# The sum of all branches in two column groups of 224 instead of four of 112, in a single-core decode kernel

## The chip, the cores and the metric

The kernel runs on one core of a Trainium2 chip. The metric is the time on the device in microseconds (us), from runs without a profile; the profile's own span is a little shorter. Before the change the median of three runs is 189.18 us (189.01 to 189.19), and the profiled execution has a span of 187.2 us.

## What is computed

One decode step: two batch rows of width 448 go through a layer normalization without weights, and then through two branches in parallel, whose results are added to the input.

```
xn  = layernorm(x)                              # x: (2, 1, 448) bf16
q   = xn @ wq                                   # 16 query heads of 256
k,v = last 4096 positions of the caches         # 8 kv heads of 256, each for 2 query heads
A   = softmax(q k^T / 16) v  @ wo               # (2, 1, 4096) @ (4096, 448)
h   = xn @ w1 + b1                              # 448 -> 1792
B   = (h * tanh(softplus(h))) @ w2              # 1792 -> 448
out = x + A + B                                 # (2, 1, 448) bf16
```

Nearly all bytes are those of the two caches: 2 batches x 8 heads x 4096 positions x 256 values in bf16 for each of k and v.

## The kernel before

**Staging.** The kernel walks over four units `u`, each of two kv heads in both batches (J = 4 streams). Per unit, two loads of 4096 KB bring k and two bring v; one of 896 KB brings the rows of `wo` that belong to the unit's heads. All big loads are issued from one queue (SyncE) in the order in which the program writes them, into a ring of three buffers. `wq`, `w1` and `w2` go through the same ring. The order of all engines is written out by hand (lines 568 to 614), with no planner.

For a unit, VectorE transposes k in 32x32 blocks (`turns`, line 269), TensorE forms the scores (line 356), ScalarE takes their exponentials (line 364), VectorE transposes them into `p` (line 367), and TensorE sums p times v (line 402). The result is gathered from its column groups (line 420), scaled by the softmax's denominator (line 447), and spread by products with a 0/1 matrix into the layout `ox` (lines 461 and 473), with which eight matmuls on `wo` add the unit's share of A to the output.

**Where the output is summed.** For units 0 to 2 these eight matmuls (`mix_early`, line 482) add into `early`, a PSUM tile of 2 x 448 that also begins with x (line 229). For the last unit everything goes into a second PSUM tile, `acc`:

- `carry` (lines 234 to 245) copies `early` to SBUF on ScalarE and brings it into `acc` with a 2x2 identity in fp32. It stands ahead of the last unit's `values`.
- `mix` (called at line 612, through `add_rows`) adds the last unit's eight rows of `wo`.
- `dense_out` adds the fourteen rows of `w2` (a "row" is here one product of a 128x2 stationary operand with 448 columns). `w2` arrives in four parts of 7, 4, 2 and 1 rows; the last three are the very last loads of the kernel.

**Column groups.** `acc` is 128 partitions x 112 columns. Row sums of two batches need only two partitions; the 448 columns are cut into G = 4 pieces of DG = 112, and piece g lies at partitions 32g and 32g+1. [...]`add_rows` (lines 247 to 256) makes four matmuls of a row, each with the same two stationary columns and another quarter of `rows`, into another column group (trace line 249).

**The end.** Four copies bring `acc` together in `res` (2 x 448, bf16): pieces 0 and 2 by VectorE (line 621), 1 and 3 by ScalarE (line 623). One transfer (line 624) writes `res` to the output, after which the program's closing synchronization runs.

Of the kernel before, what the change touches and what calls it, by code (L numbers as in the profile page):

```python
# [12 lines left out]
FP32 = mybir.dt.float32  # L13
# [4 lines left out]
def kernel(  # L18
# [14 lines left out]
    P = 128  # L33
    G = 4
# [4 lines left out]
    Bsz, Sq, D = A_x.shape  # L39
    _, Hkv, Sk, Dh = A_k_cache.shape  # L40
    HqDh = A_wq.shape[1]
    Hq = HqDh // Dh
    rep = Hq // Hkv
# [16 lines left out]
    NCH = HW // P  # L60
    F2 = F // 2
    NI = F2 // P
    DG = D // G
    assert Sq == 1 and Bsz == 2 and rep == 2 and Dh == 256 and G * DG == D and Hq == 16
    assert W == 4096 and D == 448 and F == 1792
    scale = float(Dh) ** -0.5

# [14 lines left out]
    ps_a = ctx.enter_context(tc.tile_pool(name="ps_a", bufs=1, space=PSUM))  # L82
# [146 lines left out]
    nc.tensor.matmul(  # L229
        early[:], lhsT=ident[0:Bsz, 0:Bsz], rhs=x_bf[:], start=True, stop=False  # L230
    )
    acc = ps_a.tile([P, DG], FP32)

    def carry():
        e_sb = small.tile([P, 2 * Dh], FP32, tag="vs", name="e_sb", bufs=1)[0:Bsz, 0:D]
        nc.scalar.copy(out=e_sb, in_=early[:])
        for g in range(G):
            nc.tensor.matmul(
                acc[32 * g : 32 * g + Bsz, :],
                lhsT=id2[:],  # L240
                rhs=e_sb[:, g * DG : (g + 1) * DG],
                start=True,
                stop=False,
                skip_group_check=True,
            )

    def add_rows(lhsT, rows, stop=False):
        for g in range(G):
            nc.tensor.matmul(  # L249
                acc[32 * g : 32 * g + Bsz, :],  # L250
                lhsT=lhsT,
                rhs=rows[:, g * DG : (g + 1) * DG],
                start=False,
                stop=stop,
                skip_group_check=True,
            )
# [233 lines left out]
    def mix(u):  # L490
        ox = state.pop(("ox", u))
        w = wo_t.pop(u)[:].rearrange("p k h (c d) -> p (k h c) d", c=2)
        for i in range(8):
            add_rows(ox[:, i, :], w[:, i, :])
# [65 lines left out]
    def dense_out(part):  # L560
        k, lo, hi = w2_parts[part]
        for i in range(lo, hi):
            at = k * KH + i * D
            add_rows(
                act_bf[:, i, k, :], state["w2"][:, at : at + D], stop=(k == 1 and i == NI - 1)
            )
# [34 lines left out]
    for part in range(len(w2_parts)):  # L601
        load_w2(part)
    carry()
    values(u, 0)
    values(u, 1, 40)
# [8 lines left out]
        dense_out(part)  # L614

    res = consts.tile([Bsz, D], BF16)
    for g in range(G):
        dst = res[:, g * DG : (g + 1) * DG]
        src = acc[32 * g : 32 * g + Bsz, :]
        if g % 2 == 0:  # L620
            nc.vector.tensor_copy(out=dst, in_=src)
        else:
            nc.scalar.copy(out=dst, in_=src)
# [31 lines left out]
```

The softmax here doesn't subtract the row's maximum and nothing guards it: scores larger than these inputs give would overflow.

## Time and profile before

| what | before |
|---|---|
| time, median of 3 | 189.18 us |
| profile span | 187.2 us |
| mean granted TensorE clock | 0.717 |
| bytes read from HBM | 77.67 MB, 415 GB/s over the span |
| busy: TensorE matmul, VectorE, ScalarE | 78.2, 92.7, 12.6 us |
| matmuls into `acc` in the tail | 88, from 182.01 us on |
| one of these, from start to end | 298 ns (median) |
| copy of 2x112, VectorE and ScalarE | 266 and 244 ns (mean) |
| issue of the output transfer | 185.20 us |

How to read it: busy time of an engine is the union of its instructions' times, and matmuls overlap, so the duration of one (298 ns) says little of how often one can start. The chain of waits is the profile's way back from the last instruction to what released each step. "Granted clock" is the share of TensorE's full clock that it was given; it changes in steps over the run. Stretches of time are counted in us from the start of the span.

### The profile page before, as it was taken

To read this page: it belongs to the slowest core of one execution; us is meant where nothing else is said; L and a number is where in the kernel's file an instruction comes from. 1 tells how busy PE (TensorE), PEld (TensorE's weight loads), DVE (VectorE), ACT (ScalarE), POOL (GpSimd) and SP (SyncE) were. 2 spreads that over 40 slices of the span, in tenths; PEclk is the share of its full clock that TensorE was granted. 3 is DMA by queue.
4 is the path that set the end of the run, shared out by engine and by line. 5 is a ranking of instruction groups with operands and counts; after the bars stand their busy time and mean duration, and the time that the engine had idled before them with its cause. 6 is when DMAs were issued, how large, how long until landed. Compare 5 with 4: busy or idle time off the path is not lost.

```text
span 187.2 us, 1951 instructions
## 1 busy us (share of the span) xinstructions
PE 78.2 (42%) x852; PEld 35.3 (19%) x852; DVE 92.7 (50%) x94; ACT 12.6 (7%) x27; POOL 4.9 (3%) x16
## 2 busy tenths in 40 slices
PE   0453014793219200882049002870067004855684
PEld 0211001551003000440012001420022002422283
DVE  6604397984792098038930395048920593040021
ACT  3003000101000100110000100110001000120101
POOL 8100000000000000000000000000000000000000
PEclk9999999958555855698556755897557555996555
DMA  6999999999999999999999999999999999999991
GB/s 218 420 476 441 427 434 387 454 438 448 441 427 420 403 443 404 464 434 448 441 420 424 413 441 417 451 431 448 434 434 420 413 441 427 441 413 416 417 407 42
DMA packets 4195, 77.78 MB, mean 416 GB/s; under 512 B 470, under 2 KB 732, under 8 KB 1628
## 3 DMA queue, kind: packets, MB, share of 16 engines
q1 hardware_dynamic: 4184, 77.67, 97.0%
q8 instruction: 6, 0.10, 0.2%
q14 instruction: 1, 0.01, 0.0%
q10 hardware_dynamic: 4, 0.00, 0.0%
HBM read 77.67 MB, written 0.00 MB: 415 GB/s over the span
## 4 chain that ended last, share of the span: by engine, by line
DMA 62%; PE 17%; DVE 15%; issue 3%; ACT 1%; SPq 0%; DVEq 0%
DMA v<-in_A_v_cache_dram 30%; DMA k<-in_A_k_cache_dram 15%; DVE kt L269 12%; DMA w<-in_B_w_dram 11%; DMA wq<-in_A_wq_dram 6%; PE pv L402 5%; PE sc L356 3%; PE h_ps L519 2%; PE o L420 1%; DVE p L367 1%; PE acc L249 1%; PE dn L380 1%; PE q_ps L291 1%; PE o L435 1%; DVE rec L388 1%
## 5 line engine op out<-in xcount | busy, mean ns | idle before, releaser
L269 DVE STREAM_TRANSPOSE kt<-k 128x4096 f32<-128x4096 f32 x16 | 70.1, 4420 | 33.9 <-DMA k<-in_A_k_cache_dram 33.9
L402 PE MATMUL pv<-v,p 128*32 128x512 bf16 x244 | 25.5, 590 | 72.3 <-DMA v<-in_A_v_cache_dram 72.3
L356 PE MATMUL sc<-kt,qd 128*32 128x512 bf16 x256 | 20.8, 463 | 13.3 <-DVE kt L269 13.3
L402 PEld LDWEIGHTS <-p 128*32 128x32 bf16 x244 | 9.2, 133 | 86.7 <-issue 63.4
L356 PEld LDWEIGHTS <-qd 128*32 128x32 bf16 x256 | 7.4, 109 | 25.5 <-issue 20.5
L364 ACT ACTIVATE ex<-sc 128x512 bf16<-128x512 f32 x8 | 4.8, 597 | 89.6 <-PE sc L356 89.6
L447 DVE TENSOR_TENSOR oT<-o,rec 128x16 bf16<-128x16 f32 x4 | 0.7, 174 | 20.4 <-PE o L420 18.1
L367 DVE STREAM_TRANSPOSE p<-ex 128x512 bf16<-128x512 bf16 x8 | 5.2, 690 | 10.6 <-ACT ex L364 10.6
L388 DVE TENSOR_REDUCE rec<-dn 128x8 f32<-128x512 f32 x4 | 2.8, 692 | 13.5 <-PE dn L380 13.5
L414 ACT COPY vs<-pv 128x512 f32<-128x512 f32 x4 | 2.3, 585 | 56.5 <-PE pv L402 56.5
L420 PE MATMUL o<-sel,vs 128*128 128x8 f32 x32 | 5.2, 289 | 2.1 <-ACT vs L414 2.1
L482 PE MATMUL early<-wo,ox 128*2 128x448 bf16 x24 | 5.0, 352 | 1.9 <-ACT ox L473 1.9
L420 PEld LDWEIGHTS o<-sel,vs 128*128 128x128 f32 x32 | 4.8, 228 | 4.6 <-ACT vs L414 4.6
L380 PE MATMUL dn<-p,ones 128*128 128x512 bf16 x8 | 3.2, 491 | 3.8 <-DVE p L338 3.8
L291 PE MATMUL q_ps<-wq,xs 128*32 128x512 bf16 x28 | 3.8, 623 | 2.3 <-DMA wq<-in_A_wq_dram 1.9
L519 PE MATMUL h_ps<-xs,w 128*128 128x4 bf16 x49 | 3.7, 196 | 1.3 <-DMA w<-in_B_w_dram 1.3
L345 PE MATMUL sc<-mneg,ident 128*128 128x512 bf16 x8 | 4.1, 516 | 0.0
L308 DVE COPY qT<-qt_ps 128x16 bf16<-128x16 bf16 x4 | 0.4, 165 | 7.1 <-PE qt_ps L303 7.1
L212 PE MATMUL xr_ps<-ident,xrows 2*128 2x2 bf16 x7 | 1.0, 181 | 6.7 <-DVE xrows L211 6.7
L519 PEld LDWEIGHTS <-w 128*128 128x128 bf16 x49 | 3.2, 150 | 1.5 <-DMA w<-in_B_w_dram 1.4
L482 PEld LDWEIGHTS <-ox 128*2 128x2 bf16 x24 | 1.8, 83 | 4.1 <-ACT ox L473 2.2
L212 PEld LDWEIGHTS <-xrows 2*128 2x128 bf16 x7 | 0.7, 99 | 6.9 <-DVE xrows L211 6.7
(68 smaller groups left out, 44.9 us busy)
## 6 DMA issues: line engine op xcount, KB each, us to landing
k<-in_A_k_cache_dram SPq DMA_DIRECT2D x8, 4096.0 KB, 27.9
v<-in_A_v_cache_dram SPq DMA_DIRECT2D x7, 4096.0 KB, 21.3
wq<-in_A_wq_dram SPq DMA_DIRECT2D x2, 1792.0 KB, 9.2
wo<-in_A_wo_dram SPq DMA_DIRECT2D x4, 896.0 KB, 18.9
v<-in_A_v_cache_dram SPq DMA_DIRECT2D x1, 2560.0 KB
w<-in_B_w_dram SPq DMA_DIRECT2D x1, 1568.0 KB, 21.2
v<-in_A_v_cache_dram SPq DMA_DIRECT2D x1, 1024.0 KB, 22.0
w<-in_B_w_dram SPq DMA_DIRECT2D x1, 784.0 KB, 22.2
```

What stands on the lines that cost most here:

```text
L269: nc.vector.transpose(out=kt[i][:, :, r, :, :], in_=t[:, r * KE : (r + 1) * KE].bitcast(FP32).rearrange("p (a c j) -> p a c j", c=P // (R ...
L291: nc.tensor.matmul(q_ps[32 * u : 32 * (u + 1), :], lhsT=xs[:, s, :], rhs=wq_t[s][:, u * 512 : (u + 1) * 512], start=(s == 0), stop=(s == N ...
L345: nc.tensor.matmul(sc[:].rearrange("p t c m -> p (t c m)"), lhsT=ident[:], rhs=mneg[:].rearrange("p a j -> p (a j)"), start=True, stop=Fal ...
L356: nc.tensor.matmul(sc[32 * w : 32 * (w + 1)].rearrange("p t c m -> p t (c m)"), lhsT=qd[:, u, 2 * n + e, :, :].rearrange("p g q -> p (g q) ...
L364: nc.scalar.activation(out=ex[:, :, :, i, :], in_=sc[:], func=ACT.Exp, scale=scale)
L367: nc.vector.transpose(out=p_all[:, :, h * TH : (h + 1) * TH, :].rearrange("p g t q -> p t g q"), in_=ex[:, h * TH : (h + 1) * TH].rearrang ...
L380: nc.tensor.matmul(dn[:].rearrange("p a q -> p (a q)"), lhsT=ones[:], rhs=p_run[:, i].rearrange("p t q -> p (t q)"), start=(i == 0), stop= ...
L388: nc.vector.tensor_reduce(out=rec[:], in_=dn[:].rearrange("p a q -> p q a"), axis=AXIS.X, op=ALU.add)
L402: nc.tensor.matmul(pv[32 * w : 32 * (w + 1), :, :].rearrange("p x d -> p (x d)"), lhsT=p_run[:, g, 4 * a : 4 * a + 4, :].rearrange("p t q ...
L420: nc.tensor.matmul(po[:, c, :], lhsT=sb[:, x, c::2], rhs=sel[:, x, :], start=(x == 0 and c == 0), stop=(last and x == 1), skip_group_check ...
L482: nc.tensor.matmul(early[:], lhsT=ox[:, i, :], rhs=w[:, i, :], start=False, stop=(u == U - 2 and i == 7),)
L519: nc.tensor.matmul(h_ps[:, i, :, :].rearrange("p k b -> p (k b)"), lhsT=w1_v[:, s, i, :], rhs=xs[:, s, 0 : 2 * Bsz], start=False, stop=(s ...
```

## The change

`acc` becomes 128 x 224: the 448 columns are cut into SG = 2 pieces of SD = 224, at partitions 0 and 32. `carry` and `add_rows` make two matmuls of twice the width where they made four, and two copies of 224 columns, one on VectorE and one on ScalarE, replace the four of 112. It is meant to shorten the end: fewer instructions on TensorE, and one copy on each engine instead of two in a row. What is computed, and the order in which rows are added, stay the same.

```diff
+    SG, SD = 2, D // 2
-    acc = ps_a.tile([P, DG], FP32)
+    acc = ps_a.tile([P, SD], FP32)
 
     def carry():
         e_sb = small.tile([P, 2 * Dh], FP32, tag="vs", name="e_sb", bufs=1)[0:Bsz, 0:D]
         nc.scalar.copy(out=e_sb, in_=early[:])
-        for g in range(G):
+        for g in range(SG):
             nc.tensor.matmul(
                 acc[32 * g : 32 * g + Bsz, :],
                 lhsT=id2[:],
-                rhs=e_sb[:, g * DG : (g + 1) * DG],
+                rhs=e_sb[:, g * SD : (g + 1) * SD],
...
     def add_rows(lhsT, rows, stop=False):
-        for g in range(G):
+        for g in range(SG):
             nc.tensor.matmul(
                 acc[32 * g : 32 * g + Bsz, :],
                 lhsT=lhsT,
-                rhs=rows[:, g * DG : (g + 1) * DG],
+                rhs=rows[:, g * SD : (g + 1) * SD],
...
     res = consts.tile([Bsz, D], BF16)
-    for g in range(G):
-        dst = res[:, g * DG : (g + 1) * DG]
+    for g in range(SG):
+        dst = res[:, g * SD : (g + 1) * SD]
         src = acc[32 * g : 32 * g + Bsz, :]
```

More of the change, by code (lines that the diff above doesn't have):

```diff
@@ L62 @@
     NI = F2 // P
-    DG = D // G
-    assert Sq == 1 and Bsz == 2 and rep == 2 and Dh == 256 and G * DG == D and Hq == 16
+    assert Sq == 1 and Bsz == 2 and rep == 2 and Dh == 256 and Hq == 16
     assert W == 4096 and D == 448 and F == 1792
```

## The prediction

> **What bounds the kernel now.** I read the page first, then the chain of waits, then the tail in order of time, then busy time by stretches.
>
> ```profile
> PE 78.2 (42%) x852; PEld 35.3 (19%) x852; DVE 92.7 (50%) x94; ACT 12.6 (7%) x27; POOL 4.9 (3%) x16
> ...
> PEclk9999999958555855698556755897557555996555
> DMA  6999999999999999999999999999999999999991
> ...
> HBM read 77.67 MB, written 0.00 MB: 415 GB/s over the span
> ```
>
> The DMA row is at 9 in every slice but the first and the last: until about 182 us the kernel is bound by its reads, and no work of TensorE, VectorE or ScalarE matters unless it delays a read. The change touches almost only what comes after, so the question is what the last 5 us are made of. The last three digits of PEclk are 5: in the tail the matmuls have half the clock, which I take as 1.2 GHz (why, below).
>
> The chain of waits, its last pieces in order of time (start, length, what):
>
> ```profile
> 181.69 0.19 DVE ox L473
> 181.88 0.14 issue
> 182.01 1.98 PE acc L249 x76
> 183.99 0.02 issue
> 184.01 0.57 PE acc L249 x12
> 184.58 0.25 DVE res L621
> 184.83 0.30 DVEq L650
> ```
>
> The matmuls into `acc` are the chain: 88 of them from 182.01 to 184.55, then the copies to `res`. The last piece, named by a drain, covers each engine's second copy, as the timeline shows:
>
> ```profile
> 182.01 0.92 PE L249 MATMUL acc<-wo,ox 128*2 128x112 bf16 x32 [0.36 <-DVE ox L473]
> ...
> 182.71 1.83 PE L249 MATMUL acc<-w,act_bf 128*2 128x112 bf16 x56
> ...
> 184.57 0.56 DVE L621 CAST res<-acc 2x112 bf16<-2x112 f32 x2 [2.71 <-PE acc L249]
> 184.61 0.51 ACT L623 CAST res<-acc 2x112 bf16<-2x112 f32 x2 [2.76 <-PE acc L249]
> 185.20 0.28 SPq L624 DMA_DIRECT2D out_dram<-res  x1
> ```
>
> The 32 matmuls on `wo` (8 rows of four) start in the 0.70 us from 182.01 to 182.71. Instruction by instruction, the four of a row start within 10 ns of one another and each next row 93.4 ns later (182.152, .245, .338, .432 ...). 112 columns at 1.2 GHz are 93.3 ns. So the four column groups stream at the same time, and a row of 448 columns costs the time of 112.
>
> Is the tail held by TensorE or by the last pieces of `w2`? The stretches of this line tell (length, PE busy and count, PEld busy and count, clock, DMA share, GB/s):
>
> ```profile
> 182.71:182.99 0.28, 0.28 (x24) 0.28 (x16) 0.50 0.42 160
> 182.99:183.27 0.28, 0.28 (x24) 0.28 (x16) 0.50 0.42 154
> 183.27:183.55 0.28, 0.28 (x24) 0.23 (x16) 0.50 0.32 118
> 183.55:183.83 0.28, 0.28 (x20) 0.26 (x10) 0.50 0.25 86
> 183.83:184.11 0.28, 0.26 (x16) 0.10 (x8) 0.50 0.04 13
> 184.11:184.39 0.28, 0.28 (x12) 0.16 (x5) 0.50 0.00 0
> ```
>
> Both. Up to 183.3 the rows come as fast as TensorE streams them. Then the count falls from 24 to 12 while the DMA runs out: the three small parts of `w2` land at 183.41, 183.97 and 184.24 (their semaphores), and the rows that use them start at 183.45, 184.01 and 184.28, some 40 ns after. Streamed without a wait, the 22nd row would end at 182.263 + 21 x 0.0934 = 184.22; it ends at 184.54. So 0.32 us of the tail is waiting for data, and that is all the slack that slower matmuls can use.
>
> **What the Trainium skill says.** All four places are in "TensorE: Matmul & The Clock Gate". "Back-to-back issue gap" gives columns/1.2 ns at the half clock, columns/2.4 plus 2.5 ns at the full one. The trace agrees at both ends: 93.4 ns for 112 columns here, and in the third early product at line 482, at a granted clock of 1.00, 189 ns from start to start for 448 columns in one group (448/2.4 + 2.5 = 189.2). Part 3, "The mechanism", says that products in different column tiles run at once; the four starts within 10 ns agree. Part 1, "Wait — 56ns, not 53.3ns?", puts a floor of about 25 ns from start to start under small matmuls; here starts lie 2 to 7 ns apart within a row and 23.3 ns on average, so the trace contradicts that floor for matmuls in different column groups. Part 1, "What's actually happening", says the clock is released after about 3.4 us of busy array. Of this trace: TensorE is busy almost without a gap from 174.6 to 184.6, and the clock stays at 0.50.
>
> **The change part by part.**
>
> Fewer, wider matmuls. A row becomes 2 matmuls of 224 columns in 2 groups: 44 instead of 88 in the tail, in the same 22 rows. The columns of a group double: 224/1.2 = 186.7 ns a row instead of 93.4, if the two groups stream together. No row of before has two groups, but its neighbours bound it: 448 columns in four groups cost 112 columns' time, in one group 448 columns' time. If nothing of the two overlapped, a row would cost 373 ns; if the issue of instructions were what counts, 2 x 23.3 = 47 ns. I take 187, since both neighbours follow columns per group over clock to 1%.
>
> The tail, then: `ox` is ready as before, first row at 182.01. Its 252 ns become 252 + 93 = 345, so it ends at 182.357; the 22nd ends 21 x 0.1867 = 3.92 us later, at 186.28. Where are the waits for `w2`? The part of 4 rows is wanted at row 16, at 182.01 + 15 x 0.187 = 184.81 (landed 183.41); that of 2 rows at 185.56 (183.97); the last at 185.93 (184.24). All are there, so the 0.32 us of waiting goes. From 184.54 to 186.28: **+1.74 us**, which is 22 x 0.0934 = 2.05 of extra streaming less 0.32 of slack. All on the path: nothing but these matmuls leads to the copies.
>
> Half the weight loads (44 fewer of 80 to 128 ns): they already lie beside the matmuls, since rows keep to 93.4 ns. Nothing.
>
> The copies. Each engine does one of 2x224 in place of two of 2x112. VectorE took 266 ns for 112 and, at line 324, 420 ns for 256 elements a partition from PSUM in fp32: 1.07 ns an element, so 266 + 112 x 1.07 = 386 ns. ScalarE took 244 for 112 and 521 for 448 (line 236): 0.82 an element, 336 ns. Before, the second copies end at 185.135 and 185.119, 0.563 and 0.513 after the first ones start. After, the later is VectorE, 0.386. Saved: 0.563 - 0.386 = **0.18 us**, on the path, since the output waits for both. Bounds: 0.10, if the wider copy also pays something for its width, to 0.25.
>
> `carry` (line 238): 4 fp32 products in two passes each become 2 of twice the width. It takes 0.37 us at 167.21 now; streamed in half as many groups it takes perhaps 0.2 us more. The pieces of `values` behind it on TensorE wait for `v` for 4.6 us in two waits, the longer 3.48, which leaves 1.1 for the one after `carry`. Hidden.
>
> The size of `acc` in PSUM (896 bytes a partition) is nothing in time; the output transfer is the same.
>
> Sum: +1.74 - 0.18 = +1.56 us. 189.18 + 1.56 = **190.7 us**, 0.8% slower.
>
> **The rivals.**
>
> 1. *The rows stay hidden, and the kernel is faster.* If issuing instructions sets the pace, or the landing of `w2`, the end stays at the last landing plus one row, 184.24 + 0.3, and only the copies count: 189.0. For it: the last three pieces of the tail do wait for a landing, and the starts average 23 ns. Against: the slack is 0.32 us, while doubling the stream asks 2.05; and the 93.4 ns between rows is the streaming time to the nanosecond, with gaps of 2 ns inside a row.
>
> 2. *The clock rises in the longer tail.* 4.3 us without a gap might bring it to 1.00. The clock changes in steps of 3.41 us; the next steps would fall at 183.54 and 186.95. If it rose at 183.54, the 2.74 us left would halve: 189.18 + 1.56 - 1.37 = 189.4. Against: in the 3.4 us ahead of that step the array is filled with columns far less than at 94.8 to 98.2 us, where 20 matmuls of 512 columns in four groups did not raise it; with two groups in use it is filled less still than before.
>
> 3. *Two groups don't overlap as four do*, in whole: 22 x 0.373 = 8.2 us for the rows, so 186.28 + 4.1, and 194.8 us. Against: nothing in either neighbour hints at it.
>
> **How the numbers follow.** Forecast 0.88, rival 1 0.05, rival 2 0.05, rival 3 0.02. In the forecast the spread is that of the copies (0.15 in all), some 0.1 for the fill of the first row, and 0.2 for medians of runs (the three of before lie within 0.18): 190.35 to 191.1. This leaves out the rivals, 0.12, and some 0.05 of the forecast, so it holds about 0.83. Slower by over 0.2% means over 189.56: 0.88 + 0.02 + part of rival 2 = 0.92. Within: 0.03, the rest of rival 2. Faster: 0.05, rival 1.
>
> **What would show it.** Right: 44 matmuls into `acc` in the tail, rows 187 ns apart, at a clock of 0.50 with two starts close together; no wait for `w2` between them; their end near 186.3; one copy of about 386 ns on VectorE and 336 on ScalarE. Rows 93 ns apart would refute the sum, and point to the clock or to a pace of issue; rows 373 ns apart to rival 3. A clock of 1.00 in the last two slices of the page is rival 2. The prediction fails too if the reads before 182 us take another time, which nothing in the change should cause.

## The result, and the profile after

The changed kernel takes 190.73 us (median of 6 runs, 190.08 to 191.04) against 189.12 us before (6 runs): a ratio of 1.0082, 95% interval 1.0066 to 1.0098. It is slower by 1.6 us; forecast were 190.7 us. Medians here and below are of all runs of a kernel, while ratios leave out the executions more than 1.5% above its fastest, of which only the runs with added products have any.

The page's rows for the clock and the transfers, of the changed kernel:

```profile
PEclk9999999958555855798556655896558555998555
DMA  6999999999999999999999999999999999999980
```

The clock is again at 5 in the last three slices. The DMA row now ends with an 8 and a 0: the stretch after the last read, 2.9 us before, has become nearly as long as a slice of the page (4.5 of 4.7 us).

Its tail in order of time (start, length, engine, line, operation):

```profile
182.31 1.66 PE L249 MATMUL acc<-wo,ox 128*2 128x224 bf16 x16 [0.36 <-DVE ox L473]
...
183.76 2.82 PE L249 MATMUL acc<-w,act_bf 128*2 128x224 bf16 x28
186.61 0.38 DVE L621 CAST res<-acc 2x224 bf16<-2x224 f32 x1 [4.45 <-PE acc L249]
186.65 0.34 ACT L623 CAST res<-acc 2x224 bf16<-2x224 f32 x1 [4.50 <-PE acc L249]
187.06 0.28 SPq L624 DMA_DIRECT2D out_dram<-res  x1
```

Half as many matmuls take longer: 44 from 182.312 to 186.581, 4.27 us, where 88 took 2.53. Instruction by instruction the two of a row start 2 ns apart, and rows follow every 186.7 ns (182.639, .826, 183.012, .199 ...). Nothing waits for `w2` any more. By stretches (length, PE busy and count, PEld busy and count, clock, DMA share, GB/s):

```profile
182.99:183.27 0.28, 0.28 (x8) 0.20 (x4) 0.50 0.58 221
184.11:184.39 0.28, 0.28 (x8) 0.20 (x4) 0.50 0.08 26
185.51:185.79 0.28, 0.28 (x6) 0.19 (x4) 0.50 0.00 0
```

Before, the count fell where the DMA ran out. Here the rows keep their 186.7 ns with DMA at 221 GB/s and at 0 (a count of 8 or 6 is where the stretch cuts the rows): TensorE alone sets the pace.

The two profiled spans differ by 1.86 us (187.17 and 189.03), and the time of the output's issue by as much (185.198 and 187.057). It divides almost without a rest: the first row starts 0.30 later (182.011 and 182.312), because the reads of this execution landed later (the last part of `w2` at 184.239 and 184.559); the rows take 4.269 - 2.532 = 1.74 more; from the first copy's start to the issue it is 0.443 instead of 0.626, 0.18 less. The 0.30 belongs to the execution and not to the change: in a later profile of the same changed kernel (below) the first row started at 181.975.

### The profile page after: what moved, and what is told of

Read it like the earlier page. It is cut to its first block, busy times and chain, and to the rows that moved or that the text cites. A ratio compares the mean times of both kernels' runs of the same rounds, so it can differ in the third digit from the quotient of the medians.

```text
span 189.0 us, 1853 instructions
## 1 busy us (share of the span) xinstructions
PE 80.2 (42%) x804; PEld 36.0 (19%) x804; DVE 93.0 (49%) x93; ACT 12.4 (7%) x26; POOL 4.7 (2%) x16
## 4 chain that ended last, share of the span: by engine, by line
DMA 64%; DVE 15%; PE 14%; issue 3%; SPq 1%; ACT 1%
DMA v<-in_A_v_cache_dram 32%; DMA k<-in_A_k_cache_dram 15%; DVE kt L269 12%; DMA w<-in_B_w_dram 11%; DMA wq<-in_A_wq_dram 6%; PE pv L402 4%; PE sc L356 3%; PE acc L249 2%; PE h_ps L519 2%; DVE p L367 1%; PE q_ps L291 1%; DVE rec L388 1%; PE dn L380 1%; ACT ex L364 1%; SPq L105 1%
## 5 line engine op out<-in xcount | busy, mean ns | idle before, releaser
L356 PE MATMUL sc<-kt,qd 128*32 128x512 bf16 x256 | 21.4, 471 | 13.3 <-DVE kt L269 13.3
L249 PE MATMUL acc<-w,act_bf 128*2 128x224 bf16 x28 | 2.8, 392 | 0.0
```

The source lines that it names most:

```text
L249: nc.tensor.matmul(acc[32 * g : 32 * g + Bsz, :], lhsT=lhsT, rhs=rows[:, g * SD : (g + 1) * SD], start=False, stop=stop, skip_group_check= ...
L356: nc.tensor.matmul(sc[32 * w : 32 * (w + 1)].rearrange("p t c m -> p t (c m)"), lhsT=qd[:, u, 2 * n + e, :, :].rearrange("p g q -> p (g q) ...
```

## The experiments

The theory: the rows of the tail cost *columns per group / granted clock*, and the clock is at half there. A column group is here the place, at partitions 32g, to which one matmul of a row writes; 112 columns in 93.4 ns are 1.2 columns a ns at a granted clock of 0.50, so 2.4 at 1.00. Rivals: a price per matmul or per group whatever the clock; the landing of `w2` as the true end; the copies as the larger part.

**One group of 448.**

```diff
-    SG, SD = 2, D // 2
+    SG, SD = 1, D
```

> The change carried one step further: one group of 448 columns, 22 matmuls, one copy of 448 on VectorE. My theory is time by columns per group over clock: 373 ns a row at half clock, 22 x 0.187 = 4.1 us more than two groups, and a copy of 266 + 336 x 1.07 = 0.63 us in place of 0.39: 190.73 + 4.1 + 0.24 = 195.1 us if the clock stays at 0.50 throughout. The tail is then 8 us long, and if so long a stream brings the clock up after some 5 us, it is 193 to 194. A theory of a fixed price per matmul gives less than two groups: under 190 us.

193.38 us; ratio 1.0221 (1.0207 to 1.0235). The stretches of the tail, columns as above:

```profile
184.00:187.00 3.00, 3.00 (x9) 1.01 (x8) 0.50 0.00 0
187.78:189.12 1.34, 1.34 (x7) 0.42 (x5) 1.00 0.00 0
```

At 0.50 the rows start 373 ns apart, twice the 186.7 of two groups, with half the matmuls again. At 187.78, after 5.9 us of this stream, the clock went to 1.00 and the last rows follow every 189 ns. So the time is below the 195.1 of a constant clock, within the 193 to 194 that were given for a rise. A price per matmul is refuted: 88, 44 and 22 matmuls for the same rows take 2.5, 4.3 and 7.2 us. The one copy of 448 took 614 ns (0.63 expected).

**Three rows less, with two groups and with four.** Both leave out 3 of the 8 rows of the last unit's product with `wo`; that part of the sum is not computed.

```diff
     def mix(u):
...
-        for i in range(8):
+        for i in range(5):
```

> Two column groups as in the changed kernel, but the last unit's product with wo leaves out 3 of its 8 rows (that part of the sum is not computed). My theory: the tail is a stream of 22 rows at 187 ns with no wait, so 3 rows less take 0.56 us off: 190.73 - 0.56 = 190.2 us, and all 19 rows still follow at 187 ns. If the landing of w2 held the end, nothing would be gained: 190.7 us.

> The kernel before with the same 3 rows of wo left out. My theory: in this kernel the 0.32 us of waiting for the last parts of w2 take up what 3 rows less (0.28 us) would give, since the end is the last landing and one row: 189.1 us, no change, the waits in front of the small parts growing instead. If streaming alone set the end, it would be 189.12 - 0.28 = 188.85 us.

Two groups: 190.04 us, ratio to the kernel before 1.0039 (1.0027 to 1.0051), so 0.7 us under the full change, where 0.56 was expected. Its profile has 19 rows in 3.710 us against 22 in 4.269, 0.559 less, which is 3 x 186.7 ns; its tail started late (183.13) with late reads, and this execution was the slowest of the 22 (191.08 us), so only the length is compared. The clock's row of its page shows one thing more, in its last digit:

```profile
PEclk9999999958555965555857955579559855589657
```

The 7 is a clock that rose to 1.00 at 187.12, 0.28 us after the last row had ended.

Four groups: 189.07 us, 0.9993 (0.9983 to 1.0002), no change that can be told. What the rows gave went into a longer wait, now visible in the order of time:

```profile
182.55 0.87 PE L249 MATMUL acc<-w,act_bf 128*2 128x112 bf16 x28
183.59 1.10 PE L249 MATMUL acc<-w,act_bf 128*2 128x112 bf16 x28 [0.17 <-DMA w<-in_B_w_dram]
```

The second part of `w2` landed at 183.545, and its first row began at 183.588. The same three rows are free in the kernel before and cost their full streaming time after: the tail has gone from waiting for data to being TensorE's.

**The clock raised, first try.** Products that nobody reads, in a PSUM tile that is free by then, while TensorE waits for `v`; added to the change and to the kernel before. `warm(n)` makes n of them, each 128x128 by 512 columns; its definition is left out here.

```diff
     carry()
+    warm(4)
     values(u, 0)
+    warm(14)
     values(u, 1, 40)
```

> Two column groups, with 4 products of 128x128 by 512 columns that nobody reads ahead of the last unit's first values and 14 ahead of its second ones, where TensorE waits for v (1.1 and 3.5 us). They are to keep the granted clock up into the tail. My theory: the loss is streaming at half clock, 224 columns a group; at a clock of 1.00 a row takes 93 ns, the stream falls under the landing of w2, and only the shorter copy is left: 189.12 - 0.18, about 188.9 us. If the loss is per matmul or per column group whatever the clock, it stays near 190.7 us. If the added products run at half clock they end late and delay the tail by up to 3 us; the profile would show it.

> The kernel before with the same 18 added products. My theory: the tail ends with the landing of the last part of w2 plus one row, so a higher clock brings at most the shorter last row, 0.05 us: 189.1 us. A theory in which the clock sets the end of this kernel too has 22 rows at 47 ns, and 1.0 us less for them: 188.1 us.

Two groups: 190.55 us, ratio 1.0062 (1.0048 to 1.0076), not the 188.9 expected. The profile tells why: the clock stayed up until 181.32, fell ahead of the tail, and came back at 184.73, in the midst of it:

```profile
182.00:184.70 2.70, 2.66 (x30) 1.88 (x32) 0.50 0.37 135
184.77:185.60 0.83, 0.83 (x18) 0.51 (x12) 1.00 0.00 0
```

Up to 184.7 the rows are 187 ns apart, after it 96: both values of the theory in one tail (224/1.2 and some 2.5 ns more than 224/2.4). So the price is not one per group whatever the clock. The run failed as a remedy.

Four groups: 189.91 us, 1.0044 (1.0028 to 1.006), where 189.1 was expected. Rows of 48 to 49 ns are there while the clock is up (it fell at 182.90), and they wait for `w2`. But inside the 20th row TensorE stops, waiting for no semaphore:

```profile
184.87 0.44 PE L249 MATMUL acc<-w,act_bf 128*2 128x112 bf16 x9 [0.43 <-issue]
```

From start to start the gap is 0.68 us. What it is stayed open. The DMA records show no fetch of instructions within it; the last large one ended at 183.61.

**The clock raised up to the tail.** The same, with more products where TensorE waits for the last pieces of `v`.

```diff
     gather(u, last=False)
+    warm(6)
     values_fixed(u, 1, 40, 56)
+    warm(1)
     values_fixed(u, 1, 56, TV)
```

> Two column groups and the 18 added products ahead of the values, with 6 more behind the gather and 1 between the last two pieces of values, where TensorE waits for v, so that no 3.4 us ahead of the tail are idle. Theory: at a clock of 1.00 through the tail a row takes 96 ns (as the last rows did in the run with 18 products after its clock rose), the rows meet the landing of w2 again, and the tail from its first row to the end of the last takes 2.5 to 2.6 us in place of 4.27: 189.0 us. If the clock does not hold, each row at half clock adds 0.09 us.

> The kernel before with the same 25 added products. Theory: rows of 48 ns, but the end is the landing of the last part of w2 plus a row, so 189.1 us if nothing else happens. In the run with 18 products there was a gap of 0.68 us inside a row with no semaphore waited for, which made it slower than before (189.9 us): if that gap belongs to the added instructions, it returns here, and the time is 189.8 us again.

Two groups: 189.12 us, ratio 0.9992 (0.9976 to 1.0008). With the clock up, as in the profile of one of the nine faster runs (188.79 to 189.78), the whole loss is gone. The clock's row of the page, and the tail by stretches:

```profile
PEclk9999999957555855699555755798557655899999
```

```profile
182.90:183.18 0.28, 0.28 (x12) 0.25 (x8) 1.00 0.42 160
183.18:183.46 0.28, 0.28 (x12) 0.26 (x8) 1.00 0.37 141
183.46:183.74 0.28, 0.28 (x10) 0.20 (x6) 1.00 0.40 144
183.74:184.02 0.28, 0.28 (x10) 0.25 (x8) 1.00 0.17 58
184.02:184.30 0.28, 0.26 (x8) 0.09 (x4) 1.00 0.05 16
184.30:184.58 0.28, 0.28 (x6) 0.18 (x5) 1.00 0.00 0
```

Rows are 96 ns apart, and the falling count of the kernel before is back: parts of `w2` land at 183.651, 184.214 and 184.485, and their rows start 41 or 42 ns after each. The tail lasts 2.593 us. It is no remedy to keep: in four of the 13 executions, with a lower mean clock (0.733 to 0.750 against 0.763 to 0.781), the time was over 193 us. No trace of those was taken; the expectation of the first try named the likely way, products at half clock that end late.

Four groups: 189.42 us, 1.0019 (1.0002 to 1.0036), the fastest 188.92. In its profile the clock fell at 183.14, after four rows 48 ns apart; the rest are 93.4 apart, and the first row had started only at 182.98, since the added products ended late. The gap of the first try isn't there. So this run doesn't show what four groups do with the clock up throughout.

**The changed kernel again.**

> The changed kernel itself, beside the three others on the same chip: 190.7 us, rows 187 ns apart wherever the granted clock is 0.50. In an execution where the clock rises before the tail has ended, the rows after that take 96 ns and the time is shorter by 0.09 us for each of them; such executions would be the fastest of its runs.

190.49 us (6 runs, 189.77 to 191.29), ratio 1.0073 (1.0054 to 1.0092). Its profile has rows of 186.7 ns at 0.50 throughout, and a tail of 4.268 us. All 12 runs of the changed kernel by their mean granted clock:

```
0.721  191.29                      0.738  190.50 190.56 190.64
0.725  190.49 190.53 190.82 190.82 0.746  190.08 190.08
0.729  191.04                      0.764  189.77
```

On the whole the time falls as the clock rises. In 73 runs of the kernel before, from 0.694 to 0.812, it doesn't: 188.92 at the lowest clock, 189.18 to 190.28 at the highest. The 22 runs of two groups with three rows less divide too: the five at 0.764 and above took 189.43 to 189.58 us, the others 189.82 to 191.08. That fits a tail that has come to depend on the clock. Whether the clock rose within the tail of the fast ones is not seen, as their traces weren't kept.

**Two groups, four copies.** Each engine copies its group in two halves of 112.

```diff
-        dst = res[:, g * SD : (g + 1) * SD]
-        src = acc[32 * g : 32 * g + Bsz, :]
+        for h in range(0, SD, SD // 2):
+            dst = res[:, g * SD + h : g * SD + h + SD // 2]
+            src = acc[32 * g : 32 * g + Bsz, h : h + SD // 2]
```

> Two column groups, but four copies of 112 columns, two on each engine, as before the change. My theory: the copies' part of the change is 0.18 us of gain, so undoing it gives 190.73 + 0.18 = 190.9 us, with the output transfer issued some 0.63 us after the first copy starts instead of 0.44. A rival in which the second copy is hidden gives 190.7 us.

190.69 us (4 runs, 190.41 to 190.81); 1.0081 (1.0067 to 1.0095). Too coarse for 0.2 us, but the profile has the intervals: from the first copy's start to the issue 0.507 us, where one copy each takes 0.443 and the kernel before 0.626. So undoing the copies loses 0.064 of the 0.183, and 0.12 comes from something else than their number.

```profile
186.38 0.44 DVE L622 CAST res<-acc 2x112 bf16<-2x112 f32 x2 [4.45 <-PE acc L249]
186.41 0.39 ACT L624 CAST res<-acc 2x112 bf16<-2x112 f32 x2 [4.50 <-PE acc L249]
```

Two copies of 263 and 252 ns lie in 0.44 us: the second starts 191 ns after the first, before the first has ended.

**Four groups, the last copied first.** In the kernel before each second copy waits for TensorE's semaphore once more, in the run above not. Here the order lets the wait go.

```diff
-    for g in range(G):
+    for g in reversed(range(G)):
         dst = res[:, g * DG : (g + 1) * DG]
```

> The kernel before with the four copies in the other order: groups 3 and 2 first, then 1 and 0. TensorE ends the groups in the order 0 to 3, so the second copy of each engine needs no wait of its own any more. In the run with two groups and four copies such second copies started 0.15 to 0.19 us after the first; in the kernel before, with a wait each, 0.29 and 0.27. Theory: the copies take 0.51 us from the first start to the issue of the output in place of 0.63, but start up to 0.07 us later, as group 2 and 3 are signalled 34 and 68 ns after group 0: 0.05 us less, 189.05 us. If instead the number of copies was the price, nothing changes: 189.1 us.

189.07 us; 0.9998 (0.999 to 1.0006), and 0.608 us from the first copy to the issue.

```profile
184.63 0.54 DVE L621 CAST res<-acc 2x112 bf16<-2x112 f32 x2 [2.71 <-PE acc L249]
184.67 0.50 ACT L623 CAST res<-acc 2x112 bf16<-2x112 f32 x2 [2.75 <-PE acc L249]
```

My explanation falls: without the wait the second copy still starts 282 ns after the first (294 with it), so the wait is worth some 0.02 us. What is left as the difference is the place: these two copies read different partitions, while those that overlap read the same ones, at columns that adjoin. That the partitions are what counts was not tried alone.

**Four groups, one copy an engine.** The four copies and the one transfer make room for the lines below; the lines that go are left out.

```diff
+    nc.vector.memset(acc[:], 0.0)
...
+    res = consts.tile([P, DG], BF16)
+    nc.vector.tensor_copy(out=res[0:64, :], in_=acc[0:64, :])
+    nc.scalar.copy(out=res[64:P, :], in_=acc[64:P, :])
+    flat = out.flatten_outer_dims().rearrange("b (g c) -> b g c", g=G)
+    for b, engine in enumerate((nc.sync, nc.scalar)):
+        engine.dma_start(out=flat[b], in_=res[b : b + 97 : 32, :])
```

> Four column groups of 112 as before, but one copy on each engine: VectorE takes partitions 0 to 63 (two groups) in one copy of 64x112, ScalarE partitions 64 to 127, after a memset of the PSUM tile at the start; the output goes out in two transfers, one a batch row, from two queues. My theory: streaming stays at 93 ns a row, and the copies lose the second of each pair, 0.563 - 0.266 = 0.30 us: 188.8 us. If the two transfers cost more than one, up to 0.3 us comes back: 189.1 us.

190.1 us; 1.005 (1.0036 to 1.0064): slower than before, not faster.

```profile
185.24 0.27 DVE L618 CAST res<-acc 64x112 bf16<-64x112 f32 x1 [2.78 <-PE acc L250]
185.53 0.25 ACT L619 CAST res<-acc 64x112 bf16<-64x112 f32 x1 [3.09 <-DVE res L618]
185.81 0.63 SPq L622 DMA_DIRECT2D out_dram<-res  x1
```

Two things ate the gain of 0.3 us that was expected. As the program was built, ScalarE's copy waits for VectorE's, so both lie in a row (0.57 us to the issue). And the two transfers, each of 4 partitions that lie 32 apart, take 0.63 and 0.57 us to issue, and landed 1.63 and 1.98 us after their start, against 1.14 for the single one before. The copies thus gain 0.05 us and the transfers lose 0.84, which is most of the 1.0 us in the times. In this profile the first row also began 0.59 us later than before (182.60), as `v` landed late; that is not part of this sum.

None of these versions beats the kernel before by more than its runs can tell.

## Why the prediction was right

**Which resource.** The step that decided was to take the pace between rows, columns per group over clock, as the price; 186.7 ns was forecast for two groups and measured.

**The slack.** That 0.32 us of the tail was waiting for `w2`, and could be spent once, is what makes the sum 1.74 and not 2.05. The rows' part came out at 1.74 (4.269 - 2.532), and with the copies the terms give 1.55 of the 1.61 us between the medians. The runs with three rows less show the slack itself: free with four groups, at full price with two.

**The copies.** The 0.18 was right in size (0.626 - 0.443), with 379 and 336 ns for the wider copies where 386 and 336 were worked out. Its reason was only half right: by the experiments 0.06 is the number of copies, and the rest hangs on second copies that begin only when the first has ended (32 ns after its end in the kernel before), which they don't always.

**`carry`.** Forecast some 0.2 us more, hidden behind the wait for `v`. Before:

```profile
167.21 0.37 PE L238 MATMUL acc<-e_sb,id 2*2 2x112 f32 x8 [0.67 <-ACT e_sb L236]
...
168.65 2.47 PE L402 MATMUL pv<-v,p 128*32 128x512 bf16 x32 [1.07 <-DMA v<-in_A_v_cache_dram]
```

After:

```profile
167.60 0.54 PE L238 MATMUL acc<-e_sb,id 2*2 2x224 f32 x4 [0.67 <-ACT e_sb L236]
...
168.93 1.91 PE L402 MATMUL pv<-v,p 128*32 128x512 bf16 x32 [0.78 <-DMA v<-in_A_v_cache_dram]
```

0.54 us in place of 0.37; the wait behind it went from 1.07 to 0.78.

**The rivals.** The first (hidden rows, 189.0) was refuted by the rows' pace after the last landing. The third (no overlap of two groups) is refuted by two starts 2 ns apart and a pace half that of one group. The second, a rising clock, didn't happen in either profile of the change, but that was in part luck. The argument against it holds for a step of the clock early in the tail, such as the one assumed at 183.54. The clock of these traces changes only at steps 3.41 us apart, and where they fall in the tail differs from one execution to the next. In the two profiles of the change a step came 1.71 and 1.87 us after the first row (184.03 and 183.84), without a rise, and the next after the tail's end. In the first try with added products it came 2.69 us into the tail, and in the run with three rows less, which has no added products, after all 3.7 us of it, and both times the clock rose. So rows in two groups can raise it, where the step comes late. An execution of the change whose step falls late in the tail should be faster; none was profiled. One group's longer stream raised the clock as well, and with the clock held up by added work the loss vanished.

What the prediction left out is the spread: the kernel before hid the clock behind the landing of `w2`, the changed one shows it.

## What to carry to other kernels

Where matmuls have few stationary columns (two here), count streamed columns per column group over the granted clock, not instructions: merging four groups into two halved the instructions and doubled the time of a row. Read the pace from rows that don't wait, and take what those that wait lose as slack that can be spent only once. Before pricing a tail, look at the clock that it is granted, and at where its next step falls; here the tail ran at half the full clock, where a row costs twice what it costs at 1.00.

## What was not expected of the hardware

- Rows of one, two and four column groups: 373, 187 and 93.4 ns at a clock of 0.50, and 189, 96 and 48 to 49 at 1.00. At 1.00 some 2 to 3 ns come on top of columns/2.4.
- Two copies of 112 elements from PSUM on one engine started 150 to 191 ns apart when they read the same partitions, and 259 to 294 ns apart when they read different ones, with a wait between them or without. That the partitions are the cause was not tried alone.
- Two transfers issued at once, each of 4 partitions that lie 32 apart with 224 bytes each, took 0.57 and 0.63 us to issue, where one of 2 partitions with 896 bytes takes 0.28.
- The clock rose at a step that came after 2.69 us of rows in two groups, and stayed at 0.50 at steps after 1.71 to 1.93 us of them. In the kernel before, a matmul was in flight throughout the 3.41 us up to the step at 180.11, from 177.7 on one of 8 columns, and it stayed at 0.50 too.
